# Both ends of an attention stage feeding a mixture of experts: set-up, first states and the first slots' rows put in another order

## The chip, the cores and the metric

The kernel runs on one core of one Trainium2 chip. Its time is the device time of one execution in microseconds (us). TensorE is called PE here, VectorE DVE, ScalarE ACT, GpSimd POOL and SyncE SP; SP issues most DMAs, POOL the gathers, the scatters and some stores.

## The reference

Normalised linear attention without a mask, followed by a mixture of experts in which a token can skip its expert:

```python
kv  = einsum('bhsd,bhse->bhde', k, v)              # 8 x 8 heads, 576 rows, head size 64
o   = einsum('bhsd,bhde->bhse', q, kv)
x   = o / sqrt(mean(o*o, -1) + 1e-6) * g_norm      # -> x: 4608 tokens x 512
run = x @ w_skip > 0                               # tokens that use an expert
e   = argmax(x[run] @ w_gate);  gate = softmax(...)[e]
out = x;  out[run] += gate * (relu(x[run] @ w1[e]) @ w2[e])   # 8 experts, 512 -> 1024 -> 512
```

All inputs and outputs are float32.

## The kernel before, in words

The order of the instructions on every engine is written out by hand. The program order is the order of each engine's queue, and waits between engines follow from what reads and writes which tile region.

**Set-up** (lines 143 to 326). SP issues the loads of k and v of batch 0 in halves, then q of batch 0, then k and v of batch 1, of batch 2, and q of batch 1. ACT's queue fetches the small gate and norm weights into `room`, a tile that later takes the first expert's w2. PE warms up on nine matmuls; DVE and POOL make the index tables. Five buffers `kvds` hold a batch's state, in blocks beside zero blocks. The zeros are written by memset, those of buffer 0 by DVE at the end of its set-up list (line 325), the others by POOL.

**States.** For each batch, `state` (344) forms k^T v with 18 groups of eight 64x64 matmuls, in three thirds; after the last third, ACT copies the sums into the batch's kvds buffer (359). `state_t` (362) transposes them, `state_m` (372) multiplies by the gate weights so that the gates' logits come out beside the attention, and `state_s` (380) writes the swapped copy.

**The steps.** The attention is 36 units of work (392 to 401), two for each 256 rows of a batch and four for the last rows. Step n of the loop at 829 runs `turn(n+1)` (transpose q), `root(n-1)` (Sqrt on ACT), jobs marked "early", `values(n)` (q times the state), `squares(n)` (row sums), `norm(n-1)` (reciprocal and scaling on DVE into xl), jobs marked "pe", and `finish` of unit n-1: small POOL additions that form the logits. `scale` runs the multiplication by g_norm on POOL one step late (538), and `store_x` hands the finished rows to SP, for some units half to POOL. The states of the next batch are jobs "pe" at the six steps before the batch begins (804 to 811); there, too, the loads of k, v and q of later batches are issued, jobs marked "end".

**Gating.** Tokens are gated in three groups. `choose` (576) takes a group's best expert, `rank` (607) and `number` (623) give each token a slot, as generators of which a few pieces run in every step. After the second group the experts are ordered by their counts and expert 0's weights are loaded. `early` (754) then finds the rows of expert 0's first 128 slots from the first 22 columns of tokens (`oha_k`, `row_k`) and gathers them from the output in DRAM into `xg0`. It yields its matmuls as a job for "pe" in the next step; the sums and the gather (771 to 780) follow at the end of that step.

**The end.** In step 36 (845) come `choose` of the third group, `columns` for the first 22 columns (DVE: `ohc` at 659, `bv` at 663), and the last multiplications of `scale`, which wait for that bv. The experts' pools then take over the memory of the attention's tiles, each new tile waiting for the last users of its memory. PE transposes `xg0` (`expert_in`, 965), runs `layer_1` (991) on expert 0's first slots, and in between `rank` and `number` of the third group. `settle` (728) adds up the slots' rows by matmul and two additions on DVE, first for the 22 columns and then for the other 14, whose `columns` lie in `slot_pool`. Then all other rows can be gathered (1331 to 1335), and the eight experts run one after the other.

Of the kernel before, what the change touches and what calls it, by code (L numbers as in the profile page):

```python
# [8 lines left out]
FP32 = mybir.dt.float32  # L9
# [8 lines left out]
def kernel(  # L18
# [140 lines left out]

    warm_ps = ps_q.tile([P, 512], FP32, tag="q", name="q_ps")  # L160
# [22 lines left out]
    for f in range(NF):  # L183
# [8 lines left out]
                            scalar2=None, op0=ALU.is_equal)  # L192

# [127 lines left out]
    kvds = []  # L321
    for i in range(KVD):
        t = kvd_pool.tile([P, 2, 2, 2, PK], FP32, name=f"kvd{i}")
        for r in range(2):
            (nc.vector if i < 1 else nc.gpsimd).memset(t[r * 64:(r + 1) * 64, :, :, 1 - r, :], 0.0)
        kvds.append(t)

# [16 lines left out]
    def state(b, third):  # L344

        kt, vt = kts[b], vts[b]
        for i in range(6 * third, 6 * third + 6):
# [8 lines left out]
        if third < 2:  # L356
            return
# [142 lines left out]
    def norm(n):  # L500
# [4 lines left out]
        scale(n, inverse)  # L505
# [49 lines left out]
    def store_x(nq, b, i):  # L555

        xb = xbs.pop(nq)
        if i is None:
            rows = out.rearrange("(f hf r p c) d -> f hf p r c d", f=NF, hf=2, r=2, c=C)[b]
            nc.gpsimd.dma_start(out=rows[0, :, :, C - 1, :], in_=xb[0:64, :, :])  # L560
            return lambda: nc.sync.dma_start(out=rows[1, :, :, C - 1, :], in_=xb[64:128, :, :])
# [3 lines left out]
        if i == 1:  # L565
            nc.gpsimd.dma_start(out=rows[0], in_=x[0:64, :])

        def store():
            for hf in range(i, 2):
                nc.sync.dma_start(out=rows[hf], in_=x[hf * 64:(hf + 1) * 64, :])  # L570
# [3 lines left out]
    ohbs, rks = {}, {}  # L574

    def choose(g):
# [25 lines left out]
        nc.vector.tensor_tensor(out=ohb, in0=eorder[:, :].unsqueeze(1).to_broadcast([P, nt, E]),  # L602
                                in1=fi.unsqueeze(2).to_broadcast([P, nt, E]), op=ALU.is_equal)
# [50 lines left out]
    counted = []  # L654

    def columns(t0, nt, colid, val, pieces, pool, room):
# [4 lines left out]
            in1=hi_k[:, t0:t0 + nt].unsqueeze(2).to_broadcast([P, nt, NCOL]), op=ALU.is_equal)  # L661
        bv = pool.tile([P, room, pieces, NCOL], BF16, tag="bv", name="bv")[:, 0:nt, :, :]
        counted.append(nc.vector.tensor_tensor(
            out=bv, in0=ohc.unsqueeze(2).to_broadcast([P, nt, pieces, NCOL]),
            in1=val[:, t0:t0 + nt, :].unsqueeze(3).to_broadcast([P, nt, pieces, NCOL]),
            op=ALU.mult))
        return bv

# [80 lines left out]
    xg0 = keep.tile([P, CK, DM], FP32)  # L749
    KNOWN = (ends[LAST - 1] - 2) // 4 * S  # L750
# [3 lines left out]
    def early():  # L754
# [10 lines left out]
        def put():  # L765
            for t in range(NE):
                nc.tensor.matmul(out=ps, lhsT=oha_k[:, t, :], rhs=bv[:, t, :], start=(t == 0),
                                 stop=(t == NE - 1), skip_group_check=True)
        yield put
        row = gat_pool.tile([P, 1], FP32, tag="row1", name="row1")  # L770
        nc.vector.tensor_reduce(out=row[:, :], in_=ps, axis=AX.X, op=ALU.add)
        src = keep.tile([P, 1], I32, name="src1")

        nc.vector.tensor_scalar(out=row[:, :], in0=row[:, :], scalar1=float(N), scalar2=None,
                                op0=ALU.add)
        nc.vector.scalar_tensor_tensor(out=src[:, :], in0=row[:, :], scalar=float(N), in1=row[:, :],
                                       op0=ALU.is_lt, op1=ALU.mult)
        nc.gpsimd.indirect_dma_start(
            out=xg0[:, 0, :], out_offset=None, in_=out[0:KNOWN, :],
            in_offset=bass.IndirectOffsetOnAxis(ap=src[:, 0:1], axis=0))  # L780

    load_kv(1)
    load_kv(2)
    load_q(1)


    zero = setup.tile([64, DM], FP32)
    nc.gpsimd.memset(zero[:, :], 0.0)
    for b in range(KNOWN // S // 4 * 4, KNOWN // S):
        nc.gpsimd.dma_start(  # L790
            out=out[b * S:(b + 1) * S, :].rearrange("(p c) d -> p c d", c=C)[:, C - 1, :],
            in_=zero[:, :])
# [5 lines left out]
    parts = [lambda b: state(b, 0), lambda b: state(b, 1), lambda b: state(b, 2), state_t, state_m, state_s]  # L798
    for part in parts[:5]:
        part(0)  # L800
    turn(0)
    for part in parts[5:]:
        part(0)
    for b, n in starts.items():
        if b:
            for i, part in enumerate(parts):
# [602 lines left out]
```

## Time and profile before

| | us |
|---|---|
| three runs | 398.63, 400.13, 400.14; median 400.13 |
| profiled execution | 399.31 |
| its span, first to last instruction | 397.4 |
| PE busy | 365.8 (92% of the span) |
| DVE busy | 240.7 (61%) |
| ACT busy | 144.0 (36%) |
| POOL busy | 124.9 (31%) |
| first values(0) matmul | 20.39 |
| first layer_1 matmul of expert 0 | 122.56 |
| layer_1 on expert 0's other slots | 145.94 |
| from 162 to the end: PE busy | 223.1 of 235 |

The granted clock of PE is 0.973 in the mean. DMA moves 81.70 MB, 206 GB/s over the span, and about 390 GB/s from 7 to 80 us. "Busy" counts the time in which an instruction of the engine ran; times in the rows of the timeline are in us from the first instruction. A line number is that of the kernel before.

### The profile page before, as it was taken

The page shows a single profiled execution, that of the slowest core. Times are in us where ns is not written, and L with a number is a line of the kernel's source. Part 1 is how long each engine was busy: PE and PEld are TensorE (multiplying, and loading weights), DVE is VectorE, ACT ScalarE, POOL GpSimd, SP SyncE. Part 2 cuts the span into 40 slices and gives each one's busy share as a digit, 9 for nine tenths or more (in the row PEclk, how much of TensorE's full clock was granted, in tenths as well). Part 3 has the DMA queues.
Part 4 walks back from the last instruction along what each step waited for, and adds up shares of the span by engine and source line. Part 5 has one row for each costly group of instructions (what it writes and reads, how often), then busy time and mean ns, then how long its engine had stood idle before and what let it go on. Part 6 is the DMA issues. An engine that isn't in the chain of part 4 may idle for free.

```text
span 397.4 us, 9594 instructions
## 1 busy us (share of the span) xinstructions
PE 365.8 (92%) x3822; PEld 317.8 (80%) x3822; DVE 240.7 (61%) x615; ACT 144.0 (36%) x384; POOL 124.9 (31%) x197
## 2 busy tenths in 40 slices
PE   8789999899967889999999999999999989989991
PEld 4577988799857659579879978978988978979980
DVE  2333567577884651656756657857767756868711
ACT  2265786576862212113402421421431430421410
POOL 7023677565776270133012303203303203102001
PEclk9699999999996989999999999999999999999997
DMA  8999999985795249726516354663663572611001
GB/s 296 395 391 389 343 408 403 405 262 178 239 389 142 54 136 383 262 65 228 183 73 225 105 211 116 210 225 105 206 228 104 185 246 67 210 47 55 2 2 50
DMA packets 31544, 81.70 MB, mean 206 GB/s; under 512 B 2106, under 2 KB 2114, under 8 KB 31492
## 3 DMA queue, kind: packets, MB, share of 16 engines
q1 hardware_dynamic: 27456, 68.69, 49.6%
q0 software_dynamic: 4016, 12.31, 9.1%
q8 instruction: 32, 0.52, 0.6%
q14 instruction: 20, 0.16, 0.1%
q10 hardware_dynamic: 20, 0.02, 0.0%
HBM read 66.80 MB, written 14.48 MB: 205 GB/s over the span
## 4 chain that ended last, share of the span: by engine, by line
PE 56%; issue 17%; DMA 12%; POOL 5%; DVE 5%; ACT 2%; POOLq 0%; DVEq 0%; ACTq 0%
PE bank L1074 23%; DMA out_dram<-xg,rows 8%; PE bank L1006 6%; PE o_ps L468 6%; PE sum_ps L352 4%; PE q_ps L432 4%; PE bank L995 3%; DMA xg<-out_dram,asrc 2%; POOL xb L538 2%; PE g_ps L366 2%; DMA xg<-out_dram,src 2%; POOL out_dram L1216 1%; DVE xl L508 1%; PE bank L971 1%; POOL xg L961 1%
## 5 line engine op out<-in xcount | busy, mean ns | idle before, releaser
L1084 ACT COPY p<-bank 128x128 f32<-128x128 f32 (+6 forms) x70 | 20.8, 297 | 105.4 <-PE bank L1074 103.8
L1074 PE MATMUL bank<-xt,w 128*128 128x128 f32 (+5 forms) x336 | 55.5, 288 | 0.0
L538 POOL TENSOR_TENSOR xb<-xl,g_b 128x512 f32<-128x512 f32 x36 | 42.9, 1191 | 31.8 <-DVE rs L504 27.9
L1074 PEld LDWEIGHTS bank<-xt,w 128*128 128x128 f32 x336 | 47.0, 190 | 1.9 <-DVE bank L1078 1.2
L1078 DVE TENSOR_TENSOR bank<-bank,p 128x128 f32<-128x128 f32 (+6 forms) x70 | 23.6, 337 | 39.8 <-PE bank L1074 38.1
L1216 POOL DMA_INDIRECT out_dram<-xg,rows x16 | 16.2, 1013 | 76.9 <-DVE xg L1213 75.4
L468 PE MATMUL o_ps<-kvd,qT 128*128 128x146 f32 x240 | 36.2, 291 | 2.5 <-DVE xl L508 2.2
L1074 PE MATMUL bank<-xs,s 128*128 128x128 f32 (+5 forms) x224 | 36.7, 288 | 0.0
L1006 PE MATMUL bank<-w,ht 128*32 128x128 f32 (+2 forms) x448 | 36.6, 322 | 0.0
L468 PEld LDWEIGHTS o_ps<-kvd,qT 128*128 128x128 f32 x240 | 31.8, 190 | 4.1 <-ACT sq L482 1.6
L961 POOL DMA_INDIRECT xg<-out_dram,src x15 | 16.8, 1122 | 51.7 <-DMA out_dram<-xg,rows 29.0
L1216 POOL DMA_INDIRECT out_dram<-xg,arows x8 | 9.0, 1128 | 76.4 <-DVE xg L1213 76.1
L1074 PEld LDWEIGHTS bank<-xs,s 128*128 128x128 f32 x224 | 31.1, 190 | 1.0 <-ACT p L1084 0.8
L490 DVE TENSOR_REDUCE rs<-sq 128x8 f32<-128x512 f32 x36 | 24.5, 679 | 11.6 <-ACT sq L482 11.5
L1006 PEld LDWEIGHTS bank<-w,ht 128*32 128x32 f32 (+2 forms) x448 | 20.4, 121 | 13.6 <-issue 10.9
L508 DVE TENSOR_TENSOR xl<-o_ps,rs 128x584 f32<-128x584 f32 x33 | 25.3, 767 | 4.3 <-PE o_ps L468 0.5
L1074 PE MATMUL bank<-w,ht 128*128 128x256 f32 x112 | 27.2, 386 | 0.0
L1074 PE MATMUL bank<-t,ht 128*128 128x256 f32 x112 | 27.1, 385 | 0.0
L352 PE MATMUL sum_ps<-v,k 64*64 64x64 f32 x1152 | 25.3, 230 | 1.6 <-issue 1.5
L352 PEld LDWEIGHTS sum_ps<-v,k 64*64 64x64 f32 x1152 | 21.8, 141 | 4.7 <-issue 2.9
L1074 PE MATMUL bank<-t,hs 128*128 128x256 f32 x112 | 25.3, 379 | 0.0
L995 PE MATMUL bank<-xt,w 128*128 128x128 f32 (+1 forms) x128 | 23.2, 349 | 1.0 <-ACT xt L974 0.7
(199 smaller groups left out, 673.6 us busy)
## 6 DMA issues: line engine op xcount, KB each, us to landing
w<-in_moe_w_dram SPq DMA_DIRECT2D x16, 2048.0 KB, 10.5
q<-in_q_dram SPq DMA_DIRECT2D x8, 1152.0 KB, 9.2
k<-in_k_dram SPq DMA_DIRECT2D x7, 1152.0 KB, 12.7
v<-in_v_dram SPq DMA_DIRECT2D x7, 1152.0 KB, 13.4
out_dram<-xb SPq DMA_DIRECT2D x26, 256.0 KB, 8.7
out_dram<-xb POOLq DMA_DIRECT2D x10, 256.0 KB, 6.7
k<-in_k_dram SPq DMA_DIRECT2D x2, 576.0 KB, 5.2
v<-in_v_dram SPq DMA_DIRECT2D x2, 576.0 KB, 6.2
```

The source lines that it names most:

```text
L352: nc.tensor.matmul(out=sum_ps[w * 64:(w + 1) * 64, a, u, :], lhsT=kt[r, 2 * u + w, c, :], rhs=vt[r, 2 * u + w, c, :], start=(c == 0), stop ...
L468: nc.tensor.matmul(out=ps[:, w, 0:2 * PK].rearrange("p (r k) -> p r k", r=2)[:, :, cols], lhsT=qT[:, w, a, :], rhs=kvds[b % KVD][:, u, w, ...
L490: nc.vector.tensor_reduce(out=rs[:, :, :], in_=sq[:, :, :, :].rearrange("p x y (a d) -> p x (y a) d", a=2), axis=AX.X, op=ALU.add)
L508: nc.vector.tensor_tensor(out=xl[:, :, :, :].rearrange("p x y (a k) -> p x (y a) k", a=2), in0=ps[:, :, 0:2 * PK].rearrange("p x (h k) -> ...
L538: late.append((lambda: nc.gpsimd.tensor_tensor(out=xb[:, :, 4 * u * D:(4 * u + 4) * D].rearrange("p r (w x) -> p r w x", w=2), in0=xl[:, : ...
L961: nc.gpsimd.indirect_dma_start(out=x_of(xg, off, m), out_offset=None, in_=cut_rows(m)[:, :], in_offset=bass.IndirectOffsetOnAxis(ap=idx[:, ...
L995: nc.tensor.matmul(out=hps[:, cols], lhsT=w_sb[r][0][:, dc, f * P:(f + 1) * P], rhs=xt[:, dc, cols], start=(dc == 0), stop=(dc == DC - 1))
L1006: nc.tensor.matmul(out=yps[q * m:(q + 1) * m, 0:n], lhsT=ht[:, f, off:off + m], rhs=w_sb[r][1][:, f, q * n:(q + 1) * n], start=(f == 0), s ...
L1074: nc.tensor.matmul(out=out, lhsT=lhsT(i), rhs=rhs(i), start=start and i == 0, stop=i == k - 1, skip_group_check=True)
L1078: nc.vector.tensor_tensor(out=to, in0=x, in1=y, op=ALU.add)
L1084: nc.scalar.copy(out=t, in_=x)
L1216: ins = nc.gpsimd.indirect_dma_start(out=cut_rows(m)[:, :], out_offset=bass.IndirectOffsetOnAxis(ap=rows[:, col:col + 1], axis=0), in_=x, ...
```

## The change

At the front: a first Sqrt on ACT before its first copy; the `kvds` memsets ahead of the rest of DVE's set-up; q of batch 1 loaded before k and v of batch 2; `zero`, the source of a store of zeros, placed in `room` instead of a tile of its own; `turn(0)` ahead of `state_t(0)` and `turn(1)` ahead of `state_s(0)`. The other batches' states run in portions of two to ten groups at written-out steps, with `state_t` in the next step ahead of values, `state_m` after values and `state_s` one step later; `load_kv` comes at the end of state_t's step.

At the end: `early` makes its sums and gather together with its matmuls, in a new part "mid" between values and norm. The first slots are transposed in step 35 (`first_in`, into the new `xt_first`), `scale` is left out in step 35, and in step 36 `ohc` of the first columns comes before `choose`, `scale` after choose's last instruction and `bv` after `scale`. `columns` is split for that into `hits` and `weighed`. The last stores go through SP alone. Among the experts, three PSUM banks are passed over in place of the one that held the transposes, and the last 14 columns' `columns` come after the first `settle`, in `gat_pool`.

```diff
+    root_t = setup.tile([P, 1], FP32)
+    nc.scalar.activation(out=root_t[:, :], in_=ones[:, 0:1], func=ACT.Sqrt)
...
+    kvds = []
+    for i in range(KVD):
+        t = kvd_pool.tile([P, 2, 2, 2, PK], FP32, name=f"kvd{i}")
+        for r in range(2):
+            (nc.vector if i < 1 else nc.gpsimd).memset(t[r * 64:(r + 1) * 64, :, :, 1 - r, :], 0.0)
+        kvds.append(t)
...
-    def state(b, third):
+    def state(b, some):
         kt, vt = kts[b], vts[b]
-        for i in range(6 * third, 6 * third + 6):
+        for i in some:
...
-        if third < 2:
+        if some.stop < 2 * C:
             return
...
         inverse = nc.vector.reciprocal(out=rs[:, :, :], in_=rs[:, :, :])
-        scale(n, inverse)
+        if n < NU - 1:
+            scale(n, inverse)
...
-            nc.gpsimd.dma_start(out=rows[0, :, :, C - 1, :], in_=xb[0:64, :, :])
-            return lambda: nc.sync.dma_start(out=rows[1, :, :, C - 1, :], in_=xb[64:128, :, :])
+            def store():
+                for hf in range(2):
+                    nc.sync.dma_start(out=rows[hf, :, :, C - 1, :], in_=xb[hf * 64:(hf + 1) * 64, :, :])
+            return store
...
-        if i == 1:
+        first = int(i == 1 and b < B - 1)
+        if first:
             nc.gpsimd.dma_start(out=rows[0], in_=x[0:64, :])
         def store():
-            for hf in range(i, 2):
+            for hf in range(first, 2):
...
+    xt_first = keep.tile([P, DC, P], FP32)
+    def first_in():
+        xp = ps_q.tile([P, 512], FP32, tag="q", name="q_ps")
+        xp = xp[:, :].rearrange("p (j t) -> p j t", t=P)
+        for j in range(DC):
+            nc.tensor.transpose(out=xp[:, j, :], in_=xg0[:, 0, j * P:(j + 1) * P],
+                                identity=ident[:, :])
+        nc.scalar.copy(out=xt_first[:, :, :], in_=xp)
...
-        yield put
-        row = gat_pool.tile([P, 1], FP32, tag="row1", name="row1")
...
+            row = gat_pool.tile([P, 1], FP32, tag="row1", name="row1")
+            nc.vector.tensor_reduce(out=row[:, :], in_=ps, axis=AX.X, op=ALU.add)
...
+            nc.gpsimd.indirect_dma_start(
+                out=xg0[:, 0, :], out_offset=None, in_=out[0:KNOWN, :],
+                in_offset=bass.IndirectOffsetOnAxis(ap=src[:, 0:1], axis=0))
+        yield "mid", put
     load_kv(1)
+    load_q(1)
     load_kv(2)
-    load_q(1)
-    zero = setup.tile([64, DM], FP32)
+    zero = room[0:64, 4 * DM:5 * DM]
...
+    state(0, range(2 * C))
     turn(0)
+    state_t(0)
+    state_m(0)
+    turn(1)
+    state_s(0)
+    portions = {1: (1, (10, 8)), 2: (4, (6, 6, 6)), 3: (7, (5, 6, 7)), 4: (11, (3, 4, 4, 4, 3)),
+                5: (16, (3, 2, 6, 7)), 6: (20, (4, 4, 5, 5)), 7: (24, (4, 4, 5, 5))}
...
+            at(step, "early", lambda b=b: state_t(b))
+            at(step, "pe", lambda b=b: state_m(b))
+            at(step + 1, "early" if step + 1 == n else "pe", lambda b=b: state_s(b))
+            over = step
+        at(over, "end", lambda b=b: load_kv(b + 3))
...
+    at(NU - 1, "end", first_in)
     for n in range(NU + 2):
-        if n + 1 < NU:
+        if 1 <= n < NU - 1:
             turn(n + 1)
...
             values(n)
+        jobs(n, "mid")
...
         if n == NU:
+            ohc = hits(0, NE, colid_i, gat_pool, NE)
             drain(choose(LAST))
-            first_bv = columns(0, NE, colid_i, row_k, 2, gat_pool, NE)
-            scale(NU, counted[-1])
+            scale(NU, chosen[-1])
+            first_bv = weighed(ohc, 0, NE, row_k, 2, gat_pool, NE)
...
-        expert_in(xg0, xt0, first)
-        layer_1(0, xt0, ht0, slice(0, P), range(0, 5))
+        for _ in range(3):
+            bank()
+        layer_1(0, xt_first, ht0, slice(0, P), range(0, 5))
         rank(LAST)
         drain(number(LAST))
-        layer_1(0, xt0, ht0, slice(0, P), range(5, FC))
-        last_bv = columns(NE, NT - NE, colid_i, row_k, 2, slot_pool, NT // 2)
+        layer_1(0, xt_first, ht0, slice(0, P), range(5, FC))
         settle(0, NE, first_bv)
+        last_bv = columns(NE, NT - NE, colid_i, row_k, 2, gat_pool, NE)
```

In `portions`, the first number is the step of the first portion, the tuple the number of groups in each; the step after the last portion is state_t's.

## The prediction

> **What bounds the kernel now.** I read the page first: PE is busy for 92% of the span and the chain that ended last runs mostly over PE, so time is won only where PE waits, runs slowly, or where the stage after it waits on something else. Then I asked for busy times by stage (columns: stage, stage length, then busy us and instruction count of PE, weight loads, DVE, ACT, POOL; granted clock, DMA share, GB/s).
>
> ```profile
> 7.00:13.70 6.70, 4.17 (x145) 3.65 (x146) 5.24 (x45) 1.00 (x3) 1.44 (x3) 1.00 1.05 397
> 13.70:20.40 6.70, 6.21 (x27) 4.77 (x28) 0.00 (x0) 2.32 (x7) 0.00 (x0) 0.51 1.04 393
> 20.40:31.20 10.80, 9.49 (x235) 8.43 (x234) 3.90 (x7) 6.63 (x14) 2.13 (x5) 0.99 1.05 390
> ...
> 110.00:120.00 10.00, 5.32 (x94) 4.64 (x92) 8.41 (x21) 5.86 (x14) 8.26 (x15) 0.99 1.01 384
> 120.00:130.00 10.00, 8.53 (x63) 8.16 (x64) 5.09 (x13) 1.99 (x7) 5.63 (x12) 0.67 0.44 117
> 130.00:137.00 7.00, 5.86 (x52) 4.16 (x51) 4.61 (x10) 2.56 (x5) 2.02 (x3) 1.00 0.30 77
> ```
>
> Before 13.7 PE has gaps; from 13.7 to 20.4 it works at half clock; 31 to 110 is nearly solid PE; from 110 to 137 it has gaps again. Next, who PE waited for in the first 40 us (total, times, longest), and two lines of the timeline there:
>
> ```profile
> PE g_ps L366 <- DVE kvd L325: 2.4, 1, 2.4
> PE o_ps L468 <- DVE xl L508: 0.7, 1, 0.7
> PE g_ps L366 <- POOL lp L525: 0.6, 1, 0.6
> ```
> ```profile
> 23.80 1.28 ACT L497 ACT_TABLE_LOAD   x1
> 28.75 0.77 ACT L359 COPY kvd<-sum_ps 64x256 f32<-64x256 f32 x2 [0.23 <-PE sum_ps L352]
> ```
>
> The first wait is the memset of the zero half of kvd0, last in DVE's setup list (12.31 to 13.59). The second is the table load: root(0) is late, so xl(0) and PE's values(2) are. The third is named after POOL, but what ends there are the two copies of L359: state_t right behind state costs PE 0.58 us and 0.19 more inside (1.19 us against 1.00 elsewhere), 0.77 in all. Last, the end of the attention in the timeline:
>
> ```profile
> 113.14 1.07 POOL L778 DMA_INDIRECT xg<-out_dram,src  x1 [0.78 <-DVE rs L504]
> 120.79 1.09 PE L971 MATMUL bank<-ident,xg 128*128 128x128 f32 x4 [2.54 <-DVE rs L504]
> 122.56 6.61 PE L995 MATMUL bank<-xt,w 128*128 128x128 f32 x40 [0.68 <-ACT xt L974]
> 126.27 0.27 DVE L582 TENSOR_REDUCE mx<-lg 128x14 f32<-128x112 f32 x1 [4.57 <-POOL lg L533]
> 129.97 1.19 POOL L538 TENSOR_TENSOR xb<-xl,g_b 128x512 f32<-128x512 f32 x1 [3.74 <-DVE bv L663]
> 131.46 0.66 POOL L560 DMA_DIRECT2D out_dram<-xb  x1 [0.30 <-POOL xb L538]
> 135.64 0.51 DVE L659 TENSOR_TENSOR ohc<-colid_i,hi_k 128x336 bf16<-128x336 int32 x1 [2.32 <-issue]
> 139.04 1.03 POOL L961 DMA_INDIRECT xg<-out_dram,src  x1 [6.72 <-DVE src L744]
> ```
>
> Two chains meet here. PE starts expert 0 when the first gather has landed (the trace has 120.39, 7.25 us after issue). DVE's last columns (135.64) wait, under the name "issue", for the last store: it landed at 135.36, and the chain of waits runs through xb, that store and ohc. The gather at 139.04 follows; expert 0's other slots start on PE at 145.94.
>
> [...]half clock for 6.83 us from 13.9 and from 119.7, behind windows in which PE was busy 31% and 22%; one at 54% also lost it, one at 58% did not. [...]the trace shows 1.28, and no reload for copies or squares after Sqrt's. [...] here lo_i beside an xb took 0.68 us instead of 0.17.
>
> **The front.** Removed from the path: kvd0's two memsets (2 x 0.55) move to about 1.7, where DVE idles until 7.83. The state's copies end at 12.18, so state_t could start at 12.25 and not 13.73. But turn(0) is now queued on PE ahead of it, and q(0) is the fifth load: its last packet moves at 11.65, the loads beside it land 1.1 (v's half) to 2.0 us (k1) after theirs, so q lands near 13.0. Turn(0) 13.0 to 13.6 (0.66), then state_t: no earlier than before, but turn(0) is done. PE is busy for about half of the window from 10.5 to 13.9, which I take as halved again. Then at half clock: state_t 1.6 to 15.2, kvT copy 0.4, state_m 1.0 to 16.6, turn(1) 1.1, state_s 1.2 to 18.95 (was 19.13), its copies 0.85, values(0) at 19.9 against 20.39: 0.5 us. At full clock the same list gives 17.95: 2.4 us. The rearranged portions, from 20.4 to 38: PE idled 0.73 + 0.58 + 0.19 there and some 0.3 for smaller waits (1.8 in windows of 3.4 us); after, the table load is paid at 2.2 under the first loads, and I leave 0.4 for state_t(1) and state_s(1): 1.4 us won.
>
> The loads: q1 comes two transfers (6 us) earlier, k2 and v2 3 us later (v2 near 29); their first readers are step 3 (about 28) and step 4 (about 34). The transfers hide, with 5 us to spare; if v2 were late, state(2) would wait on PE and all steps with it. load_kv moves one or two steps forward on SP, behind portions already done, so stores behind it on SP are not held. The zeros' new place costs nothing: their store (8.04 to 14.19) stays where it was on POOL.
>
> **The middle.** 1152 state matmuls remain. What is new: state_t(b) is "early", with only turn(n+1), 0.59 us, between the last portion and it. The copies need 0.77 after that portion, more if sq (0.60) and the q8 copy (0.36) are in front, as they are for short portions. The case at 49.75 gives 0.15 per batch for portions of six or more, 0.2 to 0.35 for batches 4, 6 and 7: 1.45 for six batches, and 0.3 for state_s(2), which now sits right before values(8). Evener steps win 0.3 back (PE's waits for xl in the middle). Bounds: 0, and 0.77 a batch. I take a loss of 1.45. Queued behind each such wait are values(n) and all PE work; ACT and DVE then wait for values.
>
> **The end.** The row sums and the gather (L767 to L778) move from after norm to before it in step 30: put by 109.4, three DVE steps of 0.5, gather at about 110.4 instead of 113.14, in POOL's idle 1.7 us before 110.31. DVE's squares(30) and xl(29) come 0.5 later, made up by step 31, where DVE idled 0.3 before each. With the same 7.25 it lands near 117.7, before values(35) ends at 118.25. The transposes then run at 118.3, the copy after sq(35) at 119.1, expert 0 starts at 119.7 rather than 122.56, in banks whose readers (xl(33), 118.96) are done. Five column blocks at 1.71 (half clock, to 126.5) and then 0.89 end at 127.5 (was 129.17).
> POOL loses a store issue (0.3 + 0.58) and xb(34) (1.19) before the gate sums: lg at 124.2, not 126.23; hits (0.70) fits DVE's gap of 4.57; choose takes 1.7, so ohb is there at 125.9, hidden by PE until 127.5. Rank to 128.4, number 3.2 to 131.6, layer_1's rest to 131.3, settle(0) 0.7 to 132.0. The bv of 1.26 runs beside xb(34) and xb(35): even doubled it is done by 128.5. The stores go on SP at about 128.5 and land near 132: nothing waits for them. Columns: now behind settle, 0.4 for the adds, then 0.51 + 0.86, to 133.8; covered by layer_2(0:3), 2.82 us, until 134.85 (uncovered they would cost 1.4). Settle, adds, rows: gather at 136.5 against 139.04. Through again (0.7) and two more gathers, expert 0's other slots start at 143.7 instead of 145.94: 2.2 us. If the ACT copy came late it would hold root(35) and thus the gate sums, which have 1.6 us of slack.
>
> **Sum.** 0.5 + 1.4 - 1.45 + 2.2 = 2.65 us. The profiled execution took 399.31 (span 397.4 and 1.9 around it), so 396.7; the shown runs go from 398.63 to 400.14 with the median 0.8 above the profiled one. Half of that[...]: 397.1. What follows 146 only shifts.
>
> **The rivals.** Clock kept: if q lands by 12.5[...], the front gives 2.4 and not 0.5: 395.2. For it: only 1.7 us of idle are left, against 2.4. Late gather: it lands near 120.4 as before, since SP's weights fill the queues until 116.7; expert 0 then starts as late as now, and only the freed columns are won, 1.5 instead of 2.2: 397.8. Slower: state_t stalls as in the one measured case without a turn, 0.77 x 7 = 5.4 against the 4.1 won at both ends: 401.1. It decides from 0.6 a batch; the turn of 0.59 in between speaks against it. No effect: PE's time in the middle is rearranged[...], the end gives 1: 399.
>
> **How the numbers follow.** Main case 45% (own range 395.9 to 398.4, from the middle's 0 to 2.8), clock kept 25%, late gather 12%, no effect 8%, slower 10%. A run of this kernel tells 0.5% (2.0 us) from no change: faster below 398.1. Faster: nine tenths of the main case, all of the clock case, half of late gather: 0.72. Slower (above 402.1): 0.07, the slower case with more than 0.9 a batch or another loss beside it; the rest is same. The range 393.8 to 399.7 leaves out most of the slower case and some of the clock case in which the middle also costs nothing.
>
> **What would show it.** No wait of L366 for kvd; no table load near 24; turn(0) waiting on the load of q near 13; clock after 13.9 at half or full; waits of state_t for the copies of its batch, 0.1 to 0.4 each; the first gather issued 2 to 3 us earlier against values(30) and landed before values(35) ends; the last columns released by PE or DVE instead of 2.3 us of "issue"; 2.5 us less from values(35) to the gather of expert 0's other slots. The prediction is wrong if q lands well after 13.5, if the gather still lands behind values(35), or if state_t's waits sum to over 3 us.

## The result, and the profile after

The changed kernel takes 394.51 us in the median of six runs (393.16 to 396.4), beside 400.0 us for the kernel before (398.63 to 400.4, six runs): a ratio of 0.9866 with a 95% interval of 0.9835 to 0.9897. A second comparison, beside the last experiments, gave 394.69 and 399.28 (ratio 0.9885, 0.9844 to 0.9925). It is 1.2 to 1.3% faster. The ratios leave out a run that lies more than 1.5% above the fastest of its kernel; medians and ranges take in every run. The forecast was 397.1 in a range of 393.8 to 399.7: the direction holds, the time lies inside the range, and the gain, 5.5 us between the medians, is about twice the 2.65 that the sum gave. The profiled execution took 393.16 us with a span of 391.4.

The stages of the profile after (stage, length, busy us and instructions of PE, weight loads, DVE, ACT, POOL, granted clock, DMA share, GB/s):

```profile
7.00:13.70 6.70, 5.16 (x155) 4.68 (x155) 4.15 (x43) 1.33 (x5) 1.45 (x3) 0.75 1.06 398
13.70:20.40 6.70, 5.92 (x62) 4.64 (x65) 0.90 (x3) 4.38 (x12) 0.00 (x0) 1.00 1.05 392
20.40:31.20 10.80, 8.57 (x171) 7.93 (x163) 3.88 (x7) 3.83 (x11) 3.52 (x7) 0.84 1.06 392
...
110.00:120.00 10.00, 6.98 (x112) 5.89 (x109) 8.29 (x19) 6.62 (x16) 8.16 (x15) 1.00 1.02 383
120.00:130.00 10.00, 8.40 (x93) 8.39 (x93) 8.52 (x19) 2.60 (x10) 7.76 (x12) 1.00 0.50 130
130.00:137.00 7.00, 6.62 (x50) 3.66 (x46) 4.61 (x15) 1.92 (x3) 1.05 (x1) 1.00 0.31 77
```

From 13.7 to 20.4 PE did 62 matmuls where it did 27 before, at full clock and not at half. From 120 to 130 the clock is 1.00 where it was 0.67. Who PE waited for, in the first 40 us (first two lines) and from 40 to 140 us (last two):

```profile
PE sum_ps L355 <- issue: 2.2, 1, 2.2
PE q_ps L435 <- DMA q<-in_q_dram: 1.4, 1, 1.4
```
```profile
PE bank L1034 <- ACT rs L500: 2.0, 1, 2.0
...
PE g_ps L369 <- ACT kvd L362: 0.8, 2, 0.6
```

The wait for the memset and the one behind the table load are gone. In their place turn(0) waits 1.4 us for q, state_t waits for its copies, and a stall of 2.2 us that the trace gives to no engine stands inside a portion of `state`. The timeline, front and end:

```profile
12.73 0.63 PE L435 MATMUL q_ps<-ident,q 128*128 128x128 f32 x4 [1.35 <-DMA q<-in_q_dram]
...
17.09 1.27 PE L471 MATMUL o_ps<-kvd,qT 128*128 128x146 f32 x8 [0.21 <-ACT kvd L391]
```
```profile
111.18 1.08 POOL L800 DMA_INDIRECT xg<-out_dram,src  x1 [1.80 <-DVE src L798]
118.99 0.66 PE L770 MATMUL q_ps<-ident,xg 128*128 128x128 f32 x4
121.60 4.80 PE L1034 MATMUL bank<-xt_first,w 128*128 128x128 f32 x40 [1.96 <-ACT rs L500]
124.69 0.27 DVE L589 TENSOR_REDUCE mx<-lg 128x14 f32<-128x112 f32 x1 [1.00 <-POOL lg L537]
126.48 3.30 POOL L542 TENSOR_TENSOR xb<-xl,g_b 128x512 f32<-128x512 f32 x2 [1.82 <-PE bank L1034]
132.03 0.50 DVE L665 TENSOR_TENSOR ohc<-colid_i,hi_k 128x336 bf16<-128x336 int32 x1
135.71 1.05 POOL L1000 DMA_INDIRECT xg<-out_dram,src  x1 [5.82 <-DVE src L757]
```

values(0) starts at 17.09 (before 20.39). The gather of expert 0's other rows comes at 135.71 (139.04), and the last columns (132.03) no longer wait for a store.

How the gain runs through the kernel is seen best from the start of ACT's square of a unit, then from ACT's outputs of layer_1 (times from the two profiles):

| | before | after | gain so far |
|---|---|---|---|
| square of unit 0 | 21.75 | 18.39 | 3.4 |
| square of unit 4 | 37.89 | 34.65 | 3.2 |
| square of unit 8 | 48.93 | 47.71 | 1.2 |
| square of unit 35 | 118.37 | 119.18 | -0.8 |
| first block of layer_1 out | 124.66 | 122.77 | 1.9 |
| first gather of the other rows | 139.04 | 135.71 | 3.3 |
| second block of layer_1 on them out | 150.79 | 145.31 | 5.5 |
| end | 397.4 | 391.4 | 6.1 |

The front wins 3.3 us, the middle gives back all of it and 0.8 more, and the end wins 6.3 us up to the second block and 0.6 behind it. The experiments ask which of this is the change's and which is this execution's.

### The profile page after: what moved, and what is told of

Same layout as the page of the kernel before. It is cut to its first block, busy times and chain, and to the rows that moved or that the text cites. A ratio compares the mean times of both kernels' runs of the same rounds, so it can differ in the third digit from the quotient of the medians.

```text
span 391.4 us, 9585 instructions
## 1 busy us (share of the span) xinstructions
PE 363.3 (93%) x3822; PEld 314.0 (80%) x3822; DVE 242.8 (62%) x615; ACT 143.4 (37%) x384; POOL 124.1 (32%) x194
## 4 chain that ended last, share of the span: by engine, by line
PE 66%; issue 12%; DMA 9%; POOL 5%; DVE 3%; ACT 2%; SPq 1%; POOLq 0%; DVEq 0%; ACTq 0%
PE bank L1113 33%; PE bank L1045 7%; PE o_ps L471 7%; DMA out_dram<-xg,rows 4%; PE sum_ps L355 4%; PE q_ps L435 4%; PE bank L1034 3%; PE g_ps L369 3%; DMA q<-in_q_dram 2%; POOL xb L542 2%; DMA xg<-out_dram,src 2%; PE bank L1010 2%; POOL out_dram L1255 1%; PE g_ps L387 1%; DMA xg<-out_dram,asrc 1%
## 5 line engine op out<-in xcount | busy, mean ns | idle before, releaser
L542 POOL TENSOR_TENSOR xb<-xl,g_b 128x512 f32<-128x512 f32 x36 | 43.7, 1216 | 35.5 <-DVE rs L507 33.7
L471 PE MATMUL o_ps<-kvd,qT 128*128 128x146 f32 x240 | 37.0, 296 | 1.8 <-ACT kvd L391 0.7
L493 DVE TENSOR_REDUCE rs<-sq 128x8 f32<-128x512 f32 x36 | 24.5, 682 | 17.2 <-ACT sq L485 17.1
L1045 PEld LDWEIGHTS bank<-w,ht 128*32 128x32 f32 (+2 forms) x448 | 20.4, 121 | 13.6 <-issue 10.9
L1113 PE MATMUL bank<-w,ht 128*128 128x256 f32 x112 | 27.2, 386 | 0.0
L485 ACT ACTIVATE sq<-o_ps 128x512 f32<-128x512 f32 x33 | 19.7, 597 | 15.2 <-PE o_ps L471 14.5
```

Source lines behind the costliest of these rows:

```text
L471: nc.tensor.matmul(out=ps[:, w, 0:2 * PK].rearrange("p (r k) -> p r k", r=2)[:, :, cols], lhsT=qT[:, w, a, :], rhs=kvds[b % KVD][:, u, w, ...
L485: nc.scalar.activation(out=sq[:, :, :, :], in_=heads(ps, G, G + 2 * D), func=ACT.Square)
L493: nc.vector.tensor_reduce(out=rs[:, :, :], in_=sq[:, :, :, :].rearrange("p x y (a d) -> p x (y a) d", a=2), axis=AX.X, op=ALU.add)
L542: late.append((lambda: nc.gpsimd.tensor_tensor(out=xb[:, :, 4 * u * D:(4 * u + 4) * D].rearrange("p r (w x) -> p r w x", w=2), in0=xl[:, : ...
L1045: nc.tensor.matmul(out=yps[q * m:(q + 1) * m, 0:n], lhsT=ht[:, f, off:off + m], rhs=w_sb[r][1][:, f, q * n:(q + 1) * n], start=(f == 0), s ...
L1113: nc.tensor.matmul(out=out, lhsT=lhsT(i), rhs=rhs(i), start=start and i == 0, stop=i == k - 1, skip_group_check=True)
```

## The experiments

"Before" below is the kernel before on the same chip, whose median lay between 399.28 and 399.64 in the three calls.

**The end alone.** The front and the states' schedule as before, the end as changed (`zero` stays in `room`):

```diff
-    state(0, range(2 * C))
-    turn(0)
-    state_t(0)
...
+    parts = [lambda b: state(b, range(0, 6)), lambda b: state(b, range(6, 12)),
+             lambda b: state(b, range(12, 18)), state_t, state_m, state_s]
+    for part in parts[:5]:
+        part(0)
+    turn(0)
```

> The kernel before with the end's edits alone (early sums and gather, first_in, delayed scale, stores on SP, last columns in gat_pool, zeros in room); set-up, first states and the states' schedule as before. Theory A (the end gives all of the gain, the new schedule of the states gives back what the front wins): 393 to 394.5 us, attention's last sq at 118.4, the other slots' layer_1 6 us earlier than before. Theory B (front and end each give about half, as the forecast's sum had it, and the profiled run of the changed kernel only lost its front gain by a chance stall): 397 to 398 us.

Measured 395.11 us (393.82 to 397.74), ratio 0.9901 (0.9863 to 0.994). The end carries most of the gain. The time lies 0.6 us above theory A's range and 1.9 below theory B's, and the last square came at 119.9 and not at 118.4.

**The front alone**, with the new portions, on the old end:

```diff
+    state(0, range(2 * C))
+    turn(0)
+    state_t(0)
+    state_m(0)
+    turn(1)
+    state_s(0)
+    portions = {1: (1, (10, 8)), 2: (4, (6, 6, 6)), ...
```

> The kernel before with the front's edits and the states' new portions alone. Theory A: values(0) 3 us earlier than before (2 to 3.4 where the clock stays full after 13.9), but the last sq of the attention within 1 us of before's 118.4, time 399.5 to 401. Theory B: the front's 3 us survive, 396.5 to 398.

Measured 399.36 us (396.24 to 402.44, 14 runs), ratio 0.9992 (0.9961 to 1.0024): nothing. In its trace unit 4 is 4.2 us ahead of before and unit 35 only 0.15.

**The middle on the old schedule.** All of the change, but the states of batches 3 to 7 at the six steps ahead of their batch, and batch 2 one step earlier:

```diff
+        if b > 2:
+            parts = [lambda b=b, i=i: state(b, range(6 * i, 6 * i + 6)) for i in range(3)]
+            parts += [lambda b=b, part=part: part(b) for part in (state_t, state_m, state_s)]
+            for i, part in enumerate(parts):
+                at(n - 6 + i, "pe", part)
```

> The changed kernel, with the states of batches 3 to 7 on the schedule of before (thirds at six steps before the batch, state_t, state_m and state_s each after values in a later step) and those of batch 2 one step earlier. Theory A (state_t and state_s ahead of values make PE wait for ACT's copies, 0.2 to 0.8 us each time, 2 us in all): 392 to 393 us, last sq of the attention 1.5 to 2.5 us earlier than in the changed kernel (119.2). Rival (PE is full in the middle whatever the order): 394.5, last sq within 0.5 us.

Measured 393.77 us (392.73 to 395.25), ratio 0.9868 (0.9834 to 0.9902): by itself no difference from the changed kernel that these runs can show. The last square comes at 118.54, 0.6 and 1.2 us earlier than in two profiles of the changed kernel, which is between what theory and rival expected.

**What the portions cost** is clearer from equal work: PE's instructions, each counted at its usual time in the kernel before, are summed, and the times are compared at which each profile has reached the same sum. From 16 to 37 us of work (about the first 30 to 60 us) the kernel before needs 28.45 us; five profiles with the new portions need 29.79 to 29.80 (the profile after, with half clock from 27.6 to 31, 30.62), and the old schedule inside the changed kernel 28.93. From 37 to 76 us of work it is 54.18 before, 55.13 to 55.16 with the new portions. So the portions cost 1.35 and 0.97, 2.3 us, where 1.45 was forecast.

Most of this stands in state_t. Batch 4 in the timelines before and after:

```profile
65.84 1.00 PE L366 MATMUL g_ps<-ident,kvd 128*128 128x64 f32 x8
```
```profile
66.82 1.19 PE L369 MATMUL g_ps<-ident,kvd 128*128 128x64 f32 x8 [0.58 <-ACT kvd L362]
```

In the kernel before, state_t of batches 2 to 7 takes 1.00 us and begins 0.16 before the instruction ahead of it has ended. In the profile after it takes 1.18 to 1.28 and begins later than that in every batch: its first matmul starts 0.05 to 0.15 us after ACT's first copy has ended and its third 0.05 us after the second copy (66.68 and 67.08 in batch 4). Together these delays are 3.0 us in six batches, 0.34 to 0.93 in each. The view of waits shows only two of them, because it leaves out gaps under 0.15 us.

The kernel before has, on the other side, 1.8 us of stalls in the second stretch (37 to 76 us of work) that the new portions did not have there in any of these profiles:

```profile
70.19 0.39 PE L618 MATMUL g_ps<-ohb,ones 128*128 128x72 bf16 x9 [0.59 <-issue]
76.39 0.69 PE L352 MATMUL sum_ps<-v,k 64*64 64x64 f32 x31 [1.22 <-issue]
```

(Timeline of the kernel before.) Just ahead of each the trace has a packet of 16 KB on the DMA queue named "instruction" (67.70 to 68.75 and 73.84 to 74.86). The length of these stalls varies: in the profile of the end alone and in that of the filled kernel (below), both on the old schedule, they sum to 2.4 and 2.6 us, and the second stretch takes 0.5 and 0.8 us longer than in the kernel before. Against these two the portions cost 1.9 and 1.6 us and not 2.3. This asked for a test of whether the stalls go with the load on the DMA queues.

**Free DMA queues.** The kernel before without the loads of batches 3 to 7; these batches compute with the tiles of batches 0 to 2, so the outputs are others and only the stretch up to 118 us is read:

```diff
-        if b < B:
+        if b < 3:
             kts[b] = load(kv_pool, "k", k, b)
             vts[b] = load(kv_pool, "v", v, b)
+        elif b < B:
+            kts[b], vts[b] = kts[b - 3], vts[b - 3]
```

> The kernel before with the loads of k, v and q of batches 3 to 7 left out; those batches compute with the tiles of batches 0 to 2, so the work of the engines stays and the DMA queues are nearly free from 35 us on. What is read is the stretch up to 118 us alone, since the tokens and with them the experts' counts are others. Theory (PE's stalls of 0.6 to 1.7 us near 70 and 76, which the trace puts down to no other engine, [...]): these stalls shrink below 0.3 us in all, and PE does the work between units 16 and 35 in 1.8 to 2.4 us less. Rival (the stalls belong to PE's own queue and have nothing to do with the DMA load): they stay at 0.6 to 1.7 us each.

The stretch from 60 to 80 us of the kernel before, then the same of this one:

```profile
60.00:80.00 20.00, 17.95 (x410) 16.31 (x409) 13.14 (x35) 12.69 (x32) 12.86 (x24) 1.00 1.03 401
```
```profile
60.00:80.00 20.00, 19.76 (x445) 18.35 (x448) 15.24 (x39) 14.18 (x37) 14.77 (x28) 1.00 0.37 98
```

Both stalls are gone. PE is 2.25 us ahead at 76 us of work of where it stood against before at 40, and all of that is won between 66 and 78 us; outside that stretch, from 18 to 76 us of work, the two run in step. These stalls come with full DMA queues: with nothing but the loads taken away (busy share 0.37 and not 1.03), PE no longer stands still. What PE waits for in them was not shown. Up to 118 us, eight of the fourteen profiles have 17 stalls put down to "issue", of 0.26 to 2.33 us. Each ends 1.30 to 1.54 us after the end of a 16 KB packet on the queue named "instruction". And each ends at one of four places in PE's list: counting all of PE's records in the trace, weight loads and waits included, at 705, 961, 2241 (or 2242) and 2497 (or 2498), which lie multiples of 256 apart to within one record. Full queues alone do not make a stall: five of the six profiles with the new portions have none.

The 2.2 us of "issue" in the profile after belongs to the place 705; the packet there ran from 23.65 to 24.77, and the stall ends 1.34 us after it:

```profile
26.11 0.57 PE L355 MATMUL sum_ps<-v,k 64*64 64x64 f32 x21 [2.23 <-issue]
```

**The end: the gather.** All of the change, but the row sums and the first gather a step later and the transposes among the experts:

```diff
-        yield "mid", put
+        yield put
...
-        for _ in range(3):
-            bank()
-        layer_1(0, xt_first, ht0, slice(0, P), range(0, 5))
+        expert_in(xg0, xt0, first)
+        layer_1(0, xt0, ht0, slice(0, P), range(0, 5))
```

> The changed kernel with expert 0's row sums and first gather put back behind norm in the following step, and the transposes back among the experts. Theory (the gain of the end is expert 0's earlier start on PE): the gather is issued near 113.5 and lands near 120.5, layer_1 starts at 122.5 instead of 121.6 and its five blocks end at 127.5 at full clock or 129 at half clock, so rank comes 1 to 2.6 us later and everything behind it too: 395.5 to 397. Rival (the gain is POOL's relief, which brings the third group's logits forward by 1.6 us): PE's blocks were waiting for choose anyway and little is lost, 394 to 395. A third answer, that the order at the end matters only through PE's clock, would show as a time that goes with the granted clock between 120 and 130 and not with the start of layer_1.

Measured 396.53 us (394.05 to 398.04, 11 runs), ratio 0.9918 (0.9886 to 0.9949): against the changed kernel's two comparisons 1.3 to 2.1 us of the gain fall away by the ratios, clear of the noise against the first of them (0.9866) and not against the second (0.9885). PE's timeline and one of DVE's waits:

```profile
123.67 7.18 PE L1033 MATMUL bank<-xt,w 128*128 128x128 f32 x40 [0.68 <-ACT xt L1012]
```
```profile
DVE pr L637 <- PE g_ps L626: 1.8, 1, 1.8
```

The blocks start 4.2 us after unit 35's square began and not 2.4 (121.60 against 119.18), run at half clock, and DVE's `number` waits 1.8 us for them. The half clock (122.0 to 128.8) has a share in that wait: with the end alone, at half clock from 121.7, the same wait is 2.4 us, though its blocks start 2.4 after the square.

**The end: POOL's order.** All of the change, but scale at every norm, `choose` ahead of both first columns, scale behind bv, and half of the last stores on POOL:

```diff
-        if n < NU - 1:
-            scale(n, inverse)
+        scale(n, inverse)
...
-            ohc = hits(0, NE, colid_i, gat_pool, NE)
             drain(choose(LAST))
-            scale(NU, chosen[-1])
-            first_bv = weighed(ohc, 0, NE, row_k, 2, gat_pool, NE)
+            first_bv = columns(0, NE, colid_i, row_k, 2, gat_pool, NE)
+            scale(NU, bvs[-1])
```

> The changed kernel with the multiplications by g_norm, the order of the first columns and the half stores on POOL as before; the early gather, the transposes in step 35 and the last columns behind settle stay. Theory of the two chains that meet (PE's blocks, and POOL's logits with DVE's choose): the logits of the third group come at 126.2 to 126.4 instead of 124.7, choose ends at 128 instead of 126.4, rank and number 1.7 later: 395.8 to 396.5. Rival (PE's start is what counts): 394 to 395. If this kernel and the one with the late gather lose 1.5 each, either of the two chains alone is enough to hold the end back.

Measured 394.79 us (393.44 to 397.0), ratio 0.9891 (0.9854 to 0.9928): 0.3 lost in the medians and 1.0 by the ratios, not to be told from nothing (0.2 by the ratios against the second comparison). The time is the rival's. The logits do come later (6.9 us after unit 35's square, 5.5 in the profile after), and so does the gather, by 1.1 and 1.8 us against two profiles of the changed kernel (table below), but the time does not show it. In the profile after, though not in the second profile of the changed kernel, the last xb runs beside oha, which takes 3.03 us there and 2.09 here. Here it is POOL's own store that the gather waits for:

```profile
129.72 0.66 POOL L563 DMA_DIRECT2D out_dram<-xb  x1 [0.30 <-POOL xb L541]
...
135.92 1.03 POOL L996 DMA_INDIRECT xg<-out_dram,src  x1 [5.36 <-DMA out_dram<-xb]
```

**The end: the last columns** back ahead of the first settle, in slot_pool:

```diff
-        settle(0, NE, first_bv)
-        last_bv = columns(NE, NT - NE, colid_i, row_k, 2, gat_pool, NE)
+        last_bv = columns(NE, NT - NE, colid_i, row_k, 2, slot_pool, NT // 2)
+        settle(0, NE, first_bv)
```

> The changed kernel with the last 14 columns' columns back ahead of the first settle and in slot_pool, whose memory waits for the last stores. If that wait is what the end gained from: ohc starts only after the last store has landed (near 135.3), the gather of expert 0's second piece 2 us later than in the changed kernel (135.7), time 396 to 397. If the gather waits for the same store anyhow: at most 0.7 us later, time within 0.5 us of the changed kernel.

Measured 393.29 us (392.43 to 393.64), ratio 0.9851 (0.9821 to 0.9881): not slower; if anything faster, by 1.2 in the medians and 0.6 by the ratios. DVE's timeline:

```profile
130.26 2.09 DVE L652 TENSOR_TENSOR oha_k<-row_i,lo_i 128x896 bf16<-128x896 int32 x2
132.27 0.50 DVE L665 TENSOR_TENSOR ohc<-colid_i,hi_k 128x336 bf16<-128x336 int32 x1
```

The columns start as oha ends, 1.1 us before the first of the last stores lands (133.41), although they are in slot_pool. So the move is not what freed them; the wait is gone for another reason, and of the candidates, the stores' new queue or a new place of the pool over other tiles, no run took one away alone.

**Both of these together** (the old schedule for batches 3 to 7, and the columns back):

> The changed kernel with the states of batches 3 to 7 on the schedule of before and the last columns ahead of the first settle, both together. If each alone is worth nothing or a little, the two together are within the spread of the changed kernel: 393 to 394.5. If the portions of the middle cost what the times of equal work on PE say (2 to 3 us) and no stall of PE takes their place: 391 to 392.

Measured 391.72 us (388.89 to 394.05), ratio 0.9802 (0.9757 to 0.9847). Again, on another chip, beside the changed kernel itself:

> The same kernel as in the run of the two combined, again, beside the changed kernel on the same chip: 391 to 393.5; it is a gain over the changed kernel if the difference is over 1 us.

> The changed kernel itself again, for the comparison on one chip: 393.5 to 395.

391.66 us (387.84 to 394.36), ratio 0.9797 (0.9749 to 0.9846), beside 394.69 for the changed kernel: 3 us better than it, twice. In the profile of the first of these two runs (389.88 us) the middle is ahead of before by 0.94 us at unit 35, although it has the stalls of the old schedule and its front ran at half clock from 8.9 to 22.6:

```profile
68.71 0.41 PE L626 MATMUL g_ps<-ohb,ones 128*128 128x80 bf16 x10 [0.58 <-issue]
75.46 0.69 PE L355 MATMUL sum_ps<-v,k 64*64 64x64 f32 x32 [1.77 <-issue]
```

**PE's clock at the end.** The kernel before, with 17 matmuls more whose results are not read, in PE's waits, to see what the half clock of its profile (119.7 to 126.5 and 147.0 to 150.4) costs:

```diff
+    def fill(pool, tag, count):
+        ps = pool.tile([P, 512], FP32, tag=tag, name="fill")
+        for _ in range(count):
+            nc.tensor.matmul(out=ps[:, :], lhsT=ones[:, :],
+                             rhs=ones[:, :].unsqueeze(1).to_broadcast([P, 4, P]), start=True, stop=True)
+    for n, count in ((NU - 4, 3), (NU - 2, 4), (NU - 1, 6)):
+        at(n, "end", lambda count=count: fill(ps_q, "q", count))
...
+            fill(ps_b, "bank", 2 if j == 1 else 1)
```

> The kernel before with 17 matmuls on ones added whose results nobody reads, in PE's waits at the end of the attention and among expert 0's gathers (3, 4 and 6 of them after units 32, 34 and 35, then 1, 2 and 1 behind the transposes); about 0.3 us each at full clock, shorter together than the wait that they stand in. Theory[...]: no half clock between 118 and 150, from unit 35 to expert 0's other slots 1.5 to 3 us less than the 32.4 of the kernel before, total 397 to 398.5. Rival (the clock is a side effect, the chains through the gather and the gates are what was shortened): the clock stays full there and the time is that of the kernel before, within 0.7 us.

Measured 400.38 us (398.28 to 404.45, 22 runs), ratio 1.0026 (1.0005 to 1.0047): no gain, even a loss of 0.3%. Yet up to 139.6 us the clock did what was wanted (timelines of PE, then of DVE):

```profile
124.45 4.73 PE L1004 MATMUL bank<-xt,w 128*128 128x128 f32 x40 [0.68 <-ACT xt L983]
129.02 0.38 PE L612 MATMUL g_ps<-top,ident 128*128 128x120 f32 x2
130.43 0.21 PE L615 MATMUL g_ps<-ohb,ut 128*128 128x112 bf16 x1 [1.03 <-DVE ohb L602]
```
```profile
137.99 0.51 DVE L659 TENSOR_TENSOR ohc<-colid_i,hi_k 128x336 bf16<-128x336 int32 x1 [2.29 <-DMA out_dram<-xb]
```

The five blocks take 4.7 us and not 6.6. Then PE waits 1.03 for choose, DVE 2.29 for the store, and the gather comes 20.9 us after unit 35's square, against 20.7 in the kernel before. So up to this gather the half clock of the kernel before lay in the shadow of POOL's and the store's chain. Behind it the filling failed: PE waited 2.68 us at 137, and half clock came back from 139.6 to 143.0, where theory and rival both wanted none:

```profile
137.00:150.00 13.00, 9.41 (x43) 4.79 (x42) 7.75 (x25) 1.23 (x3) 5.23 (x5) 0.87 0.20 53
```

What a full clock in that stretch is worth, this run does not tell. The same filling, 12 matmuls, in the best version:

> The changed kernel with the old schedule of states for batches 3 to 7 and the last columns ahead of the first settle, and in addition 12 matmuls on ones in PE's waits at the end of the attention and among the gathers. If PE's clock at the end costs the kernel that it is added to in some executions, its median falls by 0.5 to 1.5 against the same kernel without them (about 391) and its spread narrows; if not, it stays at the same time or 0.5 above.

Measured 390.51 us (388.51 to 392.27), ratio 0.9794 (0.9755 to 0.9833): 1.2 below the same kernel without it in the medians, inside the spread of either.

## Why the forecast was right, and where its terms were not

**The sum.** 0.5 + 1.4 - 1.45 + 2.2 had the signs right, and the time fell into the range, but the end was worth nearly twice its term, and two steps by which the forecast reached that term were wrong. The first three terms together, +0.45, were measured by the front alone as a gain of 0.3 us (0.08% of 399.6; the interval goes from -1.0 to 1.6); the fourth, +2.2, by the end alone as 4.0 us (0.99%; 2.4 to 5.5). The term that was mis-sized most is the end. Undone one by one, its parts cost 1.3 to 2.1 us (gather and transposes), 0.2 to 1.0 (POOL's order) and nothing (columns); they do not have to sum to the 4.0, and what they leave open no run gives to one edit.

**The front.** Turn(0) at 13.0 was measured at 12.73, waiting for q, as described. Whether PE ran at half clock soon after 10.5 differed between executions (full from 13.7 to 20.4 in the profile after, half from 8.9 to 22.6 in that of the two combined): in ten profiles with the new front unit 0's square came from 1.0 us later to 3.7 us earlier than in the profile of before. In the profile after values(0) began at 17.09; the forecast's list gave 17.95 for full clock. Nor do these profiles tie the half clock to how busy PE was just before: of stretches of 3.4 us, ones with PE busy 60% and 64% (profile after from 3.8, end alone from 5.7) were followed by half clock, and one with 47% (profile after from 119.8) was followed by full clock. At 16 us of equal work (about 30 us) six profiles with the new front and portions are 1.0 to 3.3 us ahead, 1.9 in the mean, which is the 0.5 + 1.4 of the forecast in sum.

**The middle.** This is the step "I take a loss of 1.45". It was too small because of its price for state_t: 0.15 us a batch, and 0.2 to 0.35 for batches 4, 6 and 7, where 0.34 to 0.38 were measured for batches 2, 3, 5 and 7, 0.65 for batch 6 and 0.93 for batch 4. By equal work the portions cost 1.6 to 2.3 us net, and 4.1 if the 1.8 us of stalls that the kernel before has there are left out; state_t is 3.0 of these 4.1. The wait of values(8) came as forecast, 0.32. The forecast counted none of PE's stalls, on either side.

**The end.** The table has, in us after the start of unit 35's square: ACT's output of layer_1's fifth block (start), ohb ready, the gather of the other rows, and the second block of layer_1 on them.

| profile | fifth block | ohb | gather | second block |
|---|---|---|---|---|
| before | 10.8 | 9.6 | 20.7 | 32.4 |
| before, filled | 8.5 | 9.7 | 20.9 | 32.3 |
| gather undone | 11.4 | 8.0 | 19.5 | 31.2 |
| POOL's order undone | 9.0 | 8.6 | 18.3 | 27.7 |
| end alone | 10.1 | 7.2 | 18.3 | 30.0 |
| after | 7.3 | 7.2 | 16.5 | 26.1 |
| after, second profile | 9.1 | 7.1 | 17.2 | 27.2 |
| columns undone | 8.8 | 7.2 | 17.0 | 27.0 |

Two chains meet at `rank`, PE's blocks and POOL's logits with choose, and the later one decides; behind it the gather follows 8.15 us later wherever the blocks are clearly last (second profile, columns, gather, end alone), and 9.3 in the profile after, where ohb is as late as they are and the last xb runs beside oha (3.03 us instead of 2.09). There the gather also starts 0.86 us after its row numbers are ready (134.85) and not 0.28 as in the second profile. Just before it POOL passes waits, at 134.75 to 134.93, and the last packet of the last stores ends at 134.19; so in that execution the stores probably still held it, where the forecast had "nothing waits for them". The forecast described this meeting and put it at 127.5 (blocks) and 125.9 (ohb). Measured were 126.4 and 126.4, in an execution whose attention ended 0.8 later. Its start of layer_1 at 119.7 was missed: the first block's PSUM bank is the one that held unit 34's sums, xl(34) ended at 121.50, and PE started at 121.60. "In banks whose readers are done" was wrong, and the clock, which the forecast kept at half there, made up for it: that the two came out within 1.1 us is luck.

The other wrong step is the reading "PE starts expert 0 when the first gather has landed". xl(34) in the kernel before, then after:

```profile
119.92 0.77 DVE L508 TENSOR_TENSOR xl<-sum_ps,rs 128x584 f32<-128x584 f32 x1
```
```profile
120.73 0.77 DVE L512 TENSOR_TENSOR xl<-sum_ps,rs 128x584 f32<-128x584 f32 x1
```

In the kernel before the gather landed at 120.39, xl(34) ended at 120.69, and the transposes started at 120.79. In twelve of the thirteen profiles besides the one without the late loads, PE's first work on an expert's bank (the transposes in the old order, layer_1 in the new) starts 0.10 us after xl(34) has ended, and in the thirteenth 0.06. So in the old order, too, PE waited for that bank last. What the new order took off the path are the transposes and the copy behind xl(34), 1.87 us from its end to layer_1 before and 0.10 after, and not the wait for the landing; the early gather is what allows the transposes to run in step 35.

The gather was forecast 2.5 us earlier. Against unit 35 it came 2.4 earlier with the end alone, 3.5 and 4.1 in the two profiles of the changed kernel. Of these, 1.2 remain with the early gather undone. The larger miss is the stretch behind it, which the forecast took over unchanged: from the gather to the second block of layer_1. It goes with the clock. It takes 11.4 to 11.8 us in five profiles that have half clock between 139 and 151 (before, filled, the end alone, the gather undone, the second run of the two combined), and 9.4 to 10.1 in the other eight, which have none there. The front alone, with the old end, is among the eight (10.1 us), so the new end as such does not shorten this stretch. About 2 of the 6.3 us that the profile's table gives to the end are therefore the chance of one execution. How often executions that were not profiled run at half clock there stays open.

**The rivals.** "Clock kept" (395.2) was the nearest in number and describes the front of the profile after, but it doesn't explain the time, so that its number came near is luck: the front alone gained nothing in 14 runs (ratio 0.9992). "Late gather" did not occur: in the profile after it landed at 118.33, 7.15 us after its issue, before values(35) had ended at 119.06. In the second profile of the changed kernel it landed at 119.94, 0.26 us behind the end of values(35). That is one of the forecast's refuting signs, but it cost nothing, since layer_1 had to wait for xl(34) until 122.11. "No effect" and "slower" fall with the intervals. The other two signs did not show clearly: with q, turn(0) began between 12.4 and 13.6 in ten profiles, and state_t's waits sum to 0.8 us in the view of waits, though to 3.0 us, the limit itself, when every delay is counted.

**The last columns.** Their move was credited with part of the 2.2 us. Undone, it costs nothing; with the old middle beside it, undoing it even brings 2 to 2.6 us (0.9802 against 0.9868). Some 1.2 us of that lie at the other end of the kernel. After the last scatter has landed, the changed kernel's span goes on for 4.3 us, and for 3.1 with the columns undone. In the first DVE works off a list of semaphore waits and stands still in it for 1.83 us, and a packet of 8 KB on another queue named "instruction" starts just after the stop begins (387.44); in the second there is no such pause. The stop is there in both profiles of the changed kernel and in the kernel before (1.83 to 2.27 us), and absent in all three profiles of the kernels with the columns back and no filling. Where it occurs in the profiles of the changed kernel and of before, it ends 1.38 to 1.40 us after the end of that packet, about as far as PE's stalls end after theirs (1.30 to 1.54). That the two belong together was not shown.

## What to carry to other kernels

Where two chains meet, shortening one wins only down to the other: in the kernel before, PE's five blocks at full clock brought the next gather no earlier (20.9 us after unit 35's square against 20.7), while the early gather with its transposes moved ahead was worth 1.3 to 2.1 us once POOL's side had been relieved. Before a wait is put down to one thing, look for what else ends just before it, and in several profiles: the distance of 0.10 us to xl(34) shows what PE waited for, where the landing of the gather only came close.

Work moved ahead in steady state should be measured at equal work and not by the waits it shows: a move with 0.8 us of listed waits at state_t delayed it by 3.0. And a version built from the parts that experiments confirm can beat the whole change: here the new front, the new end, and the old middle with the columns in their old place gave 391.7 us, 3 below the change.

## What the runs showed of the hardware

PE stood still for 0.3 to 2.3 us at a time while the DMA queues were full (1.03 to 1.06 busy share, about 400 GB/s), at places 256 records or multiples of that apart, until 1.30 to 1.54 us after a packet of 16 KB on the queue named "instruction". In the one run with the queues mostly free (0.37, 98 GB/s) it did not. DVE stood still for 1.8 to 2.3 us at the end of the program, in the changed kernel and before, until 1.4 us after a packet of 8 KB on another queue of that name. No run tried what links the stops to the packets.

The mean granted clock tells little of the time: over 160 runs of 11 kernels, each against the mean of its own kernel, 0.01 more clock goes with 0.17 us less, with a standard error of 0.15. A mean of 0.955 and one of 0.986 both occur for the kernel before. Where the half clock falls tells more: ahead of the gather of the other rows it cost the kernel before nothing (the gather came 20.7 us after unit 35's square, and 20.9 at full clock), behind it half clock goes with about 1.8 us more (11.4 to 11.8 against 9.4 to 10.1).

At the end of the attention POOL's xb and DVE's work ran side by side. In the profile after, the first of the last two xb, beside DVE's bv, took 2.15 us and bv 1.25; in the kernel before, one behind the other, they took 1.19 and 1.26. The second took 1.20 beside DVE's two oha, which took 3.03 us there and 2.09 in the kernel before. DVE's lo_i took 0.57 and 0.68 us beside an xb (after, before) and 0.17 with the end alone, where the last xb had ended.
